# Sums moved from VectorE to GpSimd, the first product begun earlier, and the first pair of token blocks without sums

## The chip, the cores and the metric

The kernel runs on one core of one Trainium2 chip. The metric is the device time of one execution in microseconds (us). The kernel before took 384.91 us in the median of its first three runs (384.22, 384.91 and 767.23; the 767.23 was the first of them, and why it was slow is not known).

## The reference

Two stages follow each other. Attention with a sigmoid in place of the softmax, on 8 batches of 12 heads, 448 positions and 64 columns:

```python
scores = scale * np.matmul(q, k.transpose(0, 1, 3, 2)) - np.log(S)
attn = 1.0 / (1.0 + np.exp(-scores))
x = np.matmul(attn, v)          # then (B, H, S, D) -> (B*S, H*D) = (3584, 768)
```

and a two-layer block on its result:

```python
h = x @ w_in                    # 768 -> 2048, "product one"
g = h * np.cos(h)
out = g @ w_out                 # 2048 -> 768, "product two"
```

## The kernel before

TensorE does the scores, attention times v (AV) and both products. ScalarE does sigmoid and cosine. VectorE brings everything out of PSUM, multiplies h by its cosine, and makes copies of layouts. GpSimd only issues the loads, which cast float32 to float16 on the way.

Product two is done by a scheme with seven products for each pair of token blocks instead of eight. It needs four sums of quarters of w_out, once, and four sums of quarters of g for each of 14 pairs of blocks (a "quad" in the code). All of them are made on VectorE:

```python
def tt(out, in0, in1, op):
    nc.vector.tensor_tensor(out=out, in0=in0, in1=in1, op=op)

def dve_gsum(i, n):                        # 128x1024, fp16, four per quad
    a11, a12, a21, a22 = g_quarters(i)
    s1, s2, s4 = g_sum
    if n == 0:   tt(s1, a21, a22, ALU.add)
    elif n == 1: tt(s2, s1, a11, ALU.subtract)
    elif n == 2: tt(a21, a11, a21, ALU.subtract)
    else:        tt(s4, a12, s2, ALU.subtract)

def dve_wsum(n): ...                       # 128x3072, fp16, four in all
```

Other instructions of VectorE read SBUF:

```python
def dve_dup(s, y):                         # second half of x, 64x896 fp16, partitions swapped
    x = xts[s % N_X]
    nc.vector.tensor_copy(out=x[64 - 64 * y : 128 - 64 * y, 1], in_=x[64 * y : 64 * y + 64, 0])

def dve_il(s, i):                          # k and q with two heads interleaved, 128x896 fp16
    nc.vector.tensor_copy(out=ri.rearrange("p j y d -> p y j d"), in_=raw)

def dve_g(b, fp, part, hslot, cslot):      # g = h * cos(h): 128x768 and smaller pieces
    nc.vector.tensor_tensor(out=..., in0=hss[hslot]..., in1=css[cslot]..., op=ALU.mult)
```

The order of the instructions on each engine is not written by hand. The program contains a small model of the engines, with a duration for each kind of job; it plays the kernel through and puts the next job on whatever engine is free in the model. Constants at its top steer it. So a change of one duration, or of the engine of one sum, reorders what follows.

## Time and profile before

| kernel before | |
|---|---|
| time, median | 384.91 us |
| span of the profiled run | 382.6 us |
| TensorE, VectorE, ScalarE, GpSimd busy | 96, 76, 66, 17% |
| first product one, first product two | 26.85 us, 97.8 us |
| real work of TensorE, priced in the prediction | 347.1 us |

A multiplication of g takes 0.95 us (128x768; 55 of them, 52.4 us).

Throughout I speak of TensorE's *lost time*: the time passed less the real work done, priced with the unit costs of the prediction (0.0473 us for a 64x448 matmul, 0.1645 for a 128x384 one).

### The profile page before, as it was taken

What the parts mean: (1) busy time and instruction counts of PE and PEld (TensorE: products, weight loads), DVE (VectorE), ACT (ScalarE), POOL (GpSimd) and SP (SyncE); (2) the same over time, 40 slices, a digit from 0 to 9 for tenths busy, and PEclk for the clock granted to TensorE, in tenths of its full rate; (3) what the DMA queues carried; (4) which work ended last, traced back from release to release, by engine and by line L of the source; (5) the groups of instructions that cost most, each with busy time, mean ns of one, the idle gap of its engine ahead of it and who ended that gap; (6) DMA issues with size and microseconds to landing.
All of it is one profiled execution on the core that took longest, in us unless ns stands there. A gap on an engine that the chain in (4) does not pass through costs nothing. (4 is left out here: it accounts for less than half of the span.)

```text
span 382.6 us, 12691 instructions
## 1 busy us (share of the span) xinstructions
PE 368.7 (96%) x5577; PEld 233.8 (61%) x5577; DVE 289.2 (76%) x492; ACT 252.9 (66%) x260; POOL 66.9 (17%) x101
## 2 busy tenths in 40 slices
PE   8999997989999999999999999999999999999995
PEld 5556664666566565576665765565666555565553
DVE  2437588999877966967969788648789987779662
ACT  4997999798958688779488880389599660134000
POOL 8676331221022022030120202020000000000000
PEclk9999998999999999999999999999999999999999
DMA  8999999599869999598499956659510303210333
GB/s 165 197 197 199 215 204 201 85 153 97 126 105 169 114 121 136 116 163 115 79 177 165 133 75 120 144 67 130 109 27 2 68 18 75 53 43 2 84 82 82
DMA packets 69894, 44.14 MB, mean 115 GB/s; under 512 B 32464, under 2 KB 69840, under 8 KB 69840
## 3 DMA queue, kind: packets, MB, share of 16 engines
q0 software_dynamic: 29936, 22.48, 44.6%
q1 hardware_dynamic: 39824, 20.76, 29.3%
q8 instruction: 43, 0.70, 0.8%
q14 instruction: 11, 0.09, 0.1%
q10 hardware_dynamic: 80, 0.10, 0.1%
HBM read 45.61 MB, written 11.01 MB: 148 GB/s over the span
## 5 line engine op out<-in xcount | busy, mean ns | idle before, releaser
L253 ACT ACTIVATE sig<-pr,lgs_t 128x896 f16<-128x896 f32 x168 | 156.2, 1014 | 63.4 <-PE pr L244 60.7
L309 PEld LDWEIGHTS <-wi 64*64 64x64 f16 x3072 | 100.3, 107 | 48.5 <-issue 6.9
L309 PE MATMUL pr<-xt,wi 64*64 64x448 f16 x2048 | 117.3, 351 | 3.6 <-DVE xt L282 2.4
L326 ACT ACTIVATE cs<-hs,pih_t 128x896 f16<-128x896 f32 x63 | 61.7, 1033 | 32.3 <-DVE hs L323 30.9
L348 DVE TENSOR_TENSOR g_ring<-hs,cs 128x128 f16<-128x128 f32 (+1 forms) x134 | 74.4, 591 | 3.4 <-ACT cs L326 3.0
L412 PEld LDWEIGHTS <-g_ring 128*128 128x128 f16 x448 | 42.8, 98 | 34.1 <-issue 6.9
L244 PE MATMUL pr<-qT,kT 64*64 64x448 f16 x672 | 59.6, 356 | 2.7 <-DVE hs L323 1.5
L323 DVE COPY hs<-pr 128x896 f32<-128x896 f32 x42 | 45.7, 1088 | 21.8 <-PE pr L309 19.1
L412 PE MATMUL bk<-wo,g_ring 128*128 128x384 f16 x336 | 59.5, 327 | 1.0 <-DVE stage L358 0.9
L309 PE MATMUL bk<-xt,wi 64*64 64x448 f16 x1024 | 60.3, 349 | 0.0
L412 PEld LDWEIGHTS <-gs 128*128 128x128 f16 x336 | 32.8, 98 | 22.1 <-issue 0.4
L177 POOL DMA_DIRECT2D vt<-in_v_dram x21 | 14.9, 709 | 174.3 <-PE pr L270 157.1
L412 PE MATMUL bk<-ws,gs 128*128 128x384 f16 x224 | 41.0, 326 | 0.0
L244 PEld LDWEIGHTS <-kT 64*64 64x64 f16 x672 | 25.1, 106 | 18.2 <-issue 7.0
L323 DVE COPY hs<-bk 128x448 f32<-128x448 f32 x42 | 24.3, 616 | 11.4 <-PE bk L309 11.4
L280 DVE CAST xt<-pr 128x896 f16<-128x896 f32 x19 | 20.7, 1089 | 11.6 <-PE pr L270 11.4
L358 DVE TENSOR_TENSOR stage<-bk,p 128x384 f32<-128x384 f32 x42 | 23.3, 554 | 7.0 <-PE bk L412 6.8
L270 PE MATMUL pr<-sig,vt 64*64 64x448 f16 x476 | 26.0, 350 | 0.0
L270 PEld LDWEIGHTS <-vt 64*64 64x64 f16 x588 | 18.8, 107 | 8.9 <-issue 0.6
L412 PE MATMUL bk<-ws,g_ring 128*128 128x384 f16 x112 | 20.5, 326 | 0.1
L412 PE MATMUL bk<-wo,gs 128*128 128x384 f16 x112 | 20.5, 326 | 0.0
L358 DVE TENSOR_TENSOR stage<-bk,stage 128x384 f32<-128x384 f32 x28 | 15.5, 553 | 5.4 <-PE bk L412 5.3
(61 smaller groups left out, 248.9 us busy)
## 6 DMA issues: line engine op xcount, KB each, us to landing
out_dram<-stage SPq DMA_DIRECT2D x111, 96.0 KB, 2.2
vt<-in_v_dram POOLq DMA_DIRECT2D x21, 224.0 KB, 4.8
kraw<-in_k_dram POOLq DMA_DIRECT2D x19, 224.0 KB, 5.5
qraw<-in_q_dram POOLq DMA_DIRECT2D x19, 224.0 KB, 6.8
wo<-in_moe_w_out_dram POOLq DMA_DIRECT2D x4, 768.0 KB, 14.1
xt<-xt SPq DMA_DIRECT2D x20, 112.0 KB, 5.7
wi<-in_moe_w_in_dram POOLq DMA_DIRECT2D x16, 128.0 KB, 7.2
wi<-in_moe_w_in_dram POOLq DMA_DIRECT2D x4, 256.0 KB, 8.0
```

The source lines that it names most:

```text
L177: nc.gpsimd.dma_start(out=vt_of(s), in_=v[b, 4 * g : 4 * g + 4].rearrange("(y x) (p j) d -> (x p) y (j d)", y=2, j=NJ),)
L244: nc.tensor.matmul(out=pairs[wd][64 * x : 64 * x + 64, y, 0:S], lhsT=kT[64 * y : 64 * y + 64, x, PT * j : PT * j + PT], rhs=qT[64 * y : 64 ...
L253: nc.scalar.activation(out=sgs[slot], in_=pairs[wd][:, :, 0:S], func=AF.Sigmoid, bias=lgs_t, scale=0.125,)
L270: nc.tensor.matmul(out=two(wd)[x][64 * y : 64 * y + 64, 0:S], lhsT=vt[64 * x : 64 * x + 64, y, D * j : D * j + D], rhs=sgs[slot][64 * x : ...
L280: nc.vector.tensor_copy(out=out, in_=pairs[wd][r0:r1, :, 0:S])
L309: nc.tensor.matmul(out=two(wd)[r][64 * m : 64 * m + 64, 0:S], lhsT=w_in_sb[c][64 * r : 64 * r + 64, h, 128 * f + 64 * m : 128 * f + 64 * m ...
L323: nc.vector.tensor_copy(out=out, in_=src)
L326: nc.scalar.activation(out=css[cslot], in_=hss[hslot], func=AF.Sin, bias=pih_t, scale=1.0)
L348: nc.vector.tensor_tensor(out=out.rearrange("p n e t -> p e n t"), in0=hss[hslot][:, :, t : t + w].rearrange("p e (n t) -> p e n t", t=min ...
L358: nc.vector.tensor_tensor(out=out, in0=in0, in1=in1, op=op)
L412: nc.tensor.matmul(out=banks[bk][:, 0:HD], lhsT=lhs[:, kk, :], rhs=rhs[:, kk, :], start=first and kk == 0, stop=kk == HF - 1, skip_group_c ...
```

## The change

Its intent has three parts. Product one of batch 0 starts over the first four heads as soon as these are there (more half jobs, w_in's pieces loaded earlier, AV in smaller pieces). The first pair of token blocks is multiplied by eight plain products, so product two can begin before the sums of w_out exist. And the sums go to GpSimd, in pieces of 128x768 for w_out and 128x512 for g, to free VectorE. A list of hand-set picks (PE_PICK, DVE_PICK) goes with it. The core of the diff:

```diff
-    M2_AT = [13, 21, 26, 31, 35, 39, 37, 45, 55, 56, 56, 64, 64, 62]
+    M2_AT = [30, 8, 22, 58, 44, 53, 14, 44, 56, 62, 59, 46, 61, 57]
-    LOADS = 'q1 v0 q2 b0 v2 v1 y1 y0 q3 x0 b1 x1 ...'
+    LOADS = 'v0 q1 y2 x0 x1 q2 v1 v4 y1 q3 y0 x2 ...'
-    N_PLAIN = 0
+    N_PLAIN = 1
-    DUP_DVE = 3
+    DUP_DVE = 4
-    HALF1 = 4
-    HALF3 = 3
-    HALF_MAX = 3
+    HALF1 = 8
+    HALF3 = 8
+    HALF_MAX = 6
+    W_POOL = True
+    W_PIECES = 4
+    G_POOL = (1, 2, 3)
+    PE_PICK = {9: 's', 28: 'm', 69: 'm', ...}
+    DVE_PICK = {62: 1, 135: 1, 153: 0, 283: 1}
-    WARM_END = 40.0
+    WARM_END = 90.0
 ... (cut)
+    def gsum(eng, i, n, m, parts):
+        k = slice(HF * m // parts, HF * (m + 1) // parts)
 ...
+        eng.tensor_tensor(out=out, in0=in0, in1=in1, op=op)
 ...
+    def pool_wsum(n, m):
 ...
+        nc.gpsimd.tensor_tensor(out=out, in0=in0, in1=in1, op=ALU.subtract)
 ...
+            if n in G_POOL:
+                for m in range(2):
+                    pool_q.append((..., lambda i=i, n=n, m=m: gsum(nc.gpsimd, i, n, m, 2), fin if m else None))
+            else:
+                dve_q.append((0, 0.61, lambda i=i, n=n: gsum(nc.vector, i, n, 0, 1), fin))
 ... (rest of the generator cut)
```

## The prediction

> **What bounds the kernel now.** I read the totals per engine first, then the slices, then TensorE's instructions in order of time.
>
> ```profile
> PE 368.7 (96%) x5577; PEld 233.8 (61%) x5577; DVE 289.2 (76%) x492; ACT 252.9 (66%) x260; POOL 66.9 (17%) x101
> PE   8999997989999999999999999999999999999995
> ACT  4997999798958688779488880389599660134000
> POOL 8676331221022022030120202020000000000000
> PEclk9999998999999999999999999999999999999999
> PE 35%; DVE 1%; issue 0%
> ```
>
> TensorE is busy nearly throughout and the chain that ended last is almost all TensorE. But "busy" counts pipelined ends and filler multiplications on the identity, so I ask instead what TensorE's real work costs. The chain, listed in order of time, gives the step from one matmul to the next:
>
> ```profile
> 251.33 1.32 PE pr L270 x28
> 259.32 9.21 PE bk L412 x56
> 308.89 1.14 PE bk L309 x24
> ```
>
> So 0.0472 us for attention times v and for product one (L309), the same for the scores (0.19 us for 4), and 9.21/56 = 0.1645 us for product two. A transpose pair in the timeline takes 0.52 us for 14. Real work: 3072 x 0.0473 + 672 x 0.0473 (scores) + 672 x 0.0472 + 784 x 0.1645 + 252 x 0.037 = 145.3 + 31.8 + 31.7 + 129.0 + 9.3 = 347.1 us. The span is 382.6 us, so some 35.5 us of TensorE are lost. Laying these costs along the timeline, I find them (to about 1 us) at: 5.0 before 5 us; 10.8 from 5 to 30 us; 1.0 from 30 to 60; 8.1 from 60 to 95; 5.4 from 95 to 378 (265 us almost without a hole); 4.3 in the tail (last eviction and store). Only the second and the fourth are worth much.
>
> 5 to 30 us: ScalarE is the limit. It does one sigmoid per 0.93 us, and per sigmoid TensorE has only its scores (0.19), its AV piece (0.19) and a share of transposes (0.15) to do; product one first appears at 26.85 us. 60 to 95 us: one hole and its aftermath, then one wait:
>
> ```profile
> 62.52 1.12 PE L309 MATMUL pr<-xt,wi 64*64 64x448 f16 x8 [2.35 <-DVE xt L282]
> 63.57 0.96 PE L201 MATMUL bk<-ident,kraw 128*64 128x128 f16 x14
> ...
> 84.59 0.38 PE L244 MATMUL pr<-qT,kT 64*64 64x448 f16 x4 [1.47 <-DVE hs L323]
> ...
> 62.50:66.00 3.50, 3.43 (x48) 2.12 (x51) 3.44 (x8) 3.27 (x4) 1.12 (x2) 0.53 1.27 202
> ```
>
> The reader sees a cast of x that stood behind multiplications of g on VectorE, TensorE idle for 2.35 us, then 3.5 us at a granted clock of 0.53 in which 14 transposes take 0.96 instead of 0.58 us. VectorE is busy for 34.72 of these 35 us: it holds four sums of w_out (1.75 us each) and the first sums of g. The wait at 84.59 stands behind one of those 1.75 us sums (78.66 to 80.4 us) and what piled up after it.
>
> **What the Trainium skill says.** "TensorE: Matmul & The Clock Gate", Part 1: TensorE falls to half clock after an idle window of about 3.4 us and needs about as much busy time to come back. The lines above agree: 2.35 us idle after thin work, then 3.5 us at 0.53. "GPSIMD Engine Reference", section 3: a two-input elementwise add of 2048 columns takes 4497 ns on GpSimd, twice VectorE. The trace before has no such instruction, so it can't agree or disagree; scaled, I estimate 1.2 us for 512 columns and 1.8 us for 768. "SBUF — State Buffer", Who interferes with whom: a VectorE instruction with two SBUF inputs, or a copy in a two-port mode, and a GpSimd instruction that reads SBUF exclude each other for the whole instruction. No run shows this yet; it is the main danger here.
>
> **The change part by part**, with the instruction order of the changed kernel built but not run.
>
> 1. Earlier product one. w_in's first pieces are loaded before later k, q and v; AV is done in small pieces; 8 instead of 4 jobs of batch 0 may start on the first four heads. In issue order the first product one now follows the 11th score instead of the 22nd, that is near 17 us instead of 26.85. Counting real work issued before the same score (ScalarE sets the pace here, so the same score is about the same time), the new order is 2.3 us ahead at scores 19 to 29 and 3.0 us at score 31. I take 3 us (of the 5.3 us lost from 15 to 30 us). Price on VectorE: 16 more copies or adds of half results, 0.62 us each, 10 us, in 20 to 60 us, where VectorE is 72% busy.
>
> 2. Sums of w_out on GpSimd: 4 x 1.75 = 7.0 us off VectorE exactly in 70 to 82 us, where it is full. 16 pieces of estimated 1.8 us = 29 us on GpSimd, which is 17% busy. The 1.47 us wait should go.
>
> 3. First pair of blocks by eight plain products: 8 more matmuls, 8 x 0.1645 = +1.3 us of TensorE. In return product two can begin before the sums exist: in the issue order after the 55th score with 13 jobs of product one done, before it was after the 68th with 17. This gives TensorE 10.5 us of work without VectorE's h copies just where it starved. With fillers now allowed to 90 us the clock should not fall either. Of the 8.1 us lost from 60 to 95, I expect 5 back.
>
> 4. Three of four g sums on GpSimd: 13 x 3 x 0.685 = 26.7 us, plus 2.7 for the pair that needs none, off VectorE. 78 pieces of 1.2 us = 94 us on GpSimd. TensorE did not wait for these sums except 0.44 us between the last quads (the eviction stands behind sums). So in the middle there is nearly nothing to win, and a new cost: the g multiplications (about 80 us on VectorE), the remaining sum (9), and the re-layout copies of q and k (11.7) want the port that GpSimd's 94 + 29 us of adds hold. GpSimd holds it some 40% of 85 to 375 us; each of about 145 such VectorE instructions then waits 0.4 x 0.6 us = 0.25 us, together 36 us of VectorE, which eats the 36 us saved. VectorE's load stays near 76%, but its delays are lumpier: an eviction of PSUM can now stand behind a 0.95 us multiplication that stands behind an add. I charge 2 us of new TensorE waits to the middle. At the end, five quads follow closely; with s1 done 1.2 us after product 5 (fifth of seven), s2, a21 and s4 come 2.4 us apart, s2 about when product 6 of the next quad wants it. That costs 0 to 0.5 us a quad in place of the 0.44.
>
> 5. Table loads of ScalarE rise from 26 to 34 (8 x 1.28 = 10 us). Up to score 42 both orders have the same two bursts of four cosines, and later ScalarE has slack (66% busy). I charge nothing.
>
> Sum: -3 (early) -5 (60 to 95) +1.3 (plain) +2 (port) = -4.7 us sure-footed; the warm clock and lighter VectorE make other small waits in 95 to 378 us (5.4 us) shrink, for which, and because such a list of hand-set picks in the diff looks tuned to a result, I add -3.5. 384.9 - 8.2 = 376.7 us.
>
> **Rivals.** (a) The port lock bites: adds delay the g multiplications, h buffers come free late, and TensorE, whose order is fixed, waits 1 us and more in each of 14 quad periods. For: VectorE at 93% or so between quads (per job of product one 1.09 + 0.95 + 0.29 us against 2.3 us of TensorE). Against: hs has 5 buffers and quads give VectorE time to catch up. Time: 382 to 390. (b) The loads don't come in time: the first w_in pieces displace q and k (at 200 GB/s the queues are full until 60 us), scores starve, the early gain vanishes: 380 to 383. (c) Both early holes close wholly and VectorE's relief shows in the middle: 10.8 + 8.1 can't go to zero before 15 us, but 4.5 + 7 + 3 - 1.3 gives 371 to 372.
>
> **Range and chances.** The sum leans on two stretches whose gain I know to about 2 us each and on a port cost of 0 to 6 us. So 370.5 to 384. The 2% line is at 377.2, right by the centre; slower by 2% needs rival (a) at over 1 us a quad.
>
> **What would show it.** Early: first product one near 17 us; the first cosine burst, now at 44.3 us, one to three us sooner. 60 to 95: clock 1.00 in every window, no wait over 1 us, first product two near 75 us instead of 97.8. Sums: GpSimd's adds at 1.2 and 1.8 us; if they show 2 us or the 128x768 multiplication rises from 0.95 to over 1.3 us, the lock is real. Middle: TensorE's lost time from 95 to the end of its work at 5 to 8 us. The prediction is wrong if the first hole stays, if TensorE waits for GpSimd inside quads, or if the lock costs over 6 us.

## More of the kernel before

The loads stand in GpSimd's own queue, in front of or behind whatever else that engine has:

```python
def load_v(s):
    nc.gpsimd.dma_start(out=vt_of(s), in_=v[b, 4 * g : 4 * g + 4].rearrange(...))
```

Up to 60 us the kernel before has lost 16.8 us, up to 100 us 25.0, up to 140 us 26.4.

The prediction shows the totals, the slices and TensorE's waits. What it does not show is the groups of VectorE's instructions by form. The columns are line, engine, operation, output and inputs, their sizes, count, then busy time and mean ns of one, then idle time before them:

```profile
L348 DVE TENSOR_TENSOR g_ring<-hs,cs 128x768 f16<-128x768 f32 x55 | 52.4, 953 | 1.6 <-ACT cs L326 1.6
L289 DVE COPY xt<-xt 64x896 f16<-64x896 f16 x28 | 12.8, 456 | 0.6
```

## The result, and the profile after

The changed kernel is correct and takes 428.35 us in the median of four runs (427.57 to 429.07). The kernel before in the same rounds took 384.71 us (the median of four with the 767.23 among them; 384.51 without it). The ratio is 1.1139, with a 95% interval of 1.1108 to 1.1169. Ratios are computed from the mean time of one kernel's runs over the mean of the other's of the same rounds, so they are not quite the ratio of the medians quoted beside them. Executions over 1.5% slower than the fastest of the same kernel are left out of the means. The change made the kernel 43.6 us slower; the prediction was 376.7 us.

The page of the changed kernel, in the views that the prediction opened with (totals, slices, and the share of the chain that ended last):

```profile
PE 379.6 (89%) x5576; PEld 237.0 (56%) x5576; DVE 322.9 (76%) x469; ACT 265.2 (62%) x268; POOL 192.0 (45%) x199
PE   8999999919729988999879969899999798999996
POOL 8776410933590936092532530826003407054472
PEclk9999999959888999999989999999999899999999
PE 14%; DVE 2%; issue 1%; ACT 0%; DVEq 0%; ACTq 0%
```

A slice is 10.7 us. TensorE has one with a tenth of work in it (85 to 96 us) and another, with 2 tenths, at 117 to 128 us; its row before had no digit below 7 but the last. These stand at GpSimd's first long trains of sums. VectorE lost 23 of its 492 instructions and yet is busy 33.7 us longer. The chain that ended last covers 17% of the span, where it covered 36% before, and TensorE's part of it falls from 35 to 14%.

The chain in order of time shows that the unit costs of TensorE did not change (9.21/56 = 0.1645 us) and what stands between:

```profile
357.11 1.14 DVE xt L296
358.26 1.25 DVE xt L296
...
370.73 9.21 PE bk L426 x56
```

Two copies of x, which took 0.46 us on average before, take 1.14 and 1.25 us and release the next product.

VectorE's groups by form, to be read against the two lines of the kernel before:

```profile
L355 DVE TENSOR_TENSOR g_ring<-hs,cs 128x768 f16<-128x768 f32 x53 | 58.8, 1109 | 0.4 <-ACT cs L333 0.3
L296 DVE COPY xt<-xt 64x896 f16<-64x896 f16 x40 | 48.6, 1214 | 0.9
```

The copies went from 12.8 to 48.6 us, far more than the 12 added ones explain, and the multiplications went from 0.953 to 1.109 us each. A mean hides which copies these are. The instructions in order of time tell it; first TensorE's, then VectorE's, then GpSimd's, around the empty slice (the columns are start, length, engine, line, operation, count, and in brackets the idle time before it and its releaser):

```profile
79.63 5.38 PE L441 MATMUL bk<-wo,g_ring 128*128 128x384 f16 x32
94.03 6.18 PE L441 MATMUL bk<-wo,g_ring 128*128 128x384 f16 x26 [9.02 <-DVE stage L450]
```

```profile
76.55 1.16 DVE L330 COPY hs<-bk 128x448 f32<-128x448 f32 x2
77.73 11.90 DVE L296 COPY xt<-xt 64x896 f16<-64x896 f16 x2
89.67 0.39 DVE L236 COPY ri<-kraw 128x896 f16<-128x896 f16 x1
```

```profile
77.07 0.71 POOL L148 DMA_DIRECT2D qraw<-in_q_dram  x1
77.78 6.44 POOL L409 TENSOR_TENSOR ws<-wo,wo 128x768 f16<-128x768 f16 x4
84.18 4.81 POOL L409 TENSOR_TENSOR ws<-wo,ws 128x768 f16<-128x768 f16 x3
```

GpSimd issues the last of three loads and then makes seven sums of w_out without a gap, until 89.0 us. A pair of copies that VectorE begins at 77.73 us ends at 89.63. The next copy within SBUF, of 128x896 and with GpSimd idle, takes 0.39 us. Behind the pair, in VectorE's queue, stands the eviction (the copy of a finished product out of PSUM) that would free a PSUM bank, so TensorE does one burst of plain products at 79.63 us and then stands still for 9.02 us. The windows (length, busy time and count of TensorE, its weight loads, VectorE, ScalarE, GpSimd, then granted clock, share of the transfers and GB/s) show the aftermath:

```profile
80.00:90.00 10.00, 5.01 (x31) 2.91 (x30) 9.96 (x4) 4.03 (x5) 8.99 (x6) 0.87 0.16 23
90.00:100.00 10.00, 5.97 (x26) 3.09 (x26) 8.81 (x18) 4.23 (x4) 0.00 (x0) 0.61 0.49 85
```

The clock, which the change wanted to keep up in just this stretch, falls to 0.61. Two more holes of this kind follow: 2.69 us at 111.38 us, behind a pair of copies of 6.35 us, and 7.90 us at 128.02 us, behind a pair of 11.1 us, of which one copy takes 10.7. TensorE's lost time goes from 21.1 us (up to 80 us) to 46.9 us (up to 140 us), and from there it creeps to 73.8 us (up to 400 us), where the kernel before has 29.8 at 360 us. The creeping part looks different. Here is VectorE, and TensorE behind it, beside the sums of g of one quad (the middle pair of GpSimd's six sums takes 3.03 us there, against 2.27 us where VectorE leaves it alone):

```profile
213.00 3.06 DVE L355 TENSOR_TENSOR g_ring<-hs,cs 128x128 f16<-128x128 f32 x2
```

```profile
217.11 0.57 PE L251 MATMUL pr<-qT,kT 64*64 64x448 f16 x4 [2.70 <-DVE hs L330]
```

The group is a multiplication of 128x128 and one of 128x768, which take 1.24 and 1.90 us here; the means before are 0.29 and 0.95 us. Each is longer by 0.95 us, a little less than one sum (1.14 us where nothing disturbs it). TensorE waits 2.70 us for the h copy behind them.

### The profile page after: what moved, and what is told of

Read it like the earlier page. It is cut to its first block, busy times and chain, and to the rows that moved or that the text cites. A ratio compares the mean times of both kernels' runs of the same rounds, so it can differ in the third digit from the quotient of the medians.

```text
span 427.0 us, 12797 instructions
## 1 busy us (share of the span) xinstructions
PE 379.6 (89%) x5576; PEld 237.0 (56%) x5576; DVE 322.9 (76%) x469; ACT 265.2 (62%) x268; POOL 192.0 (45%) x199
## 5 line engine op out<-in xcount | busy, mean ns | idle before, releaser
L260 ACT ACTIVATE sig<-pr,lgs_t 128x896 f16<-128x896 f32 x154 | 145.3, 1010 | 62.5 <-PE pr L251 62.3
L316 PE MATMUL pr<-xt,wi 64*64 64x448 f16 x1856 | 106.7, 353 | 2.3 <-DVE xt L296 1.4
L355 DVE TENSOR_TENSOR g_ring<-hs,cs 128x128 f16<-128x128 f32 (+2 forms) x130 | 90.5, 728 | 1.4 <-ACT cs L333 1.2
L390 POOL TENSOR_TENSOR gs<-gs,g_ring 128x512 f16<-128x512 f16 x26 | 33.1, 1288 | 121.2 <-DVE gs L390 81.3
L316 PE MATMUL bk<-xt,wi 64*64 64x448 f16 x1216 | 73.9, 356 | 10.3 <-DVE xt L296 7.9
L251 PE MATMUL pr<-qT,kT 64*64 64x448 f16 x672 | 63.7, 360 | 13.6 <-DVE hs L330 11.1
L330 DVE COPY hs<-pr 128x896 f32<-128x896 f32 x37 | 40.2, 1087 | 19.8 <-PE pr L316 19.4
L296 DVE COPY xt<-xt 64x896 f16<-64x896 f16 x40 | 48.6, 1214 | 0.9
L330 DVE COPY hs<-bk 128x448 f32<-128x448 f32 x48 | 27.6, 617 | 12.5 <-PE bk L316 12.5
L390 POOL TENSOR_TENSOR g_ring<-g_ring 128x512 f16<-128x512 f16 x26 | 32.2, 1256 | 0.0
L390 POOL TENSOR_TENSOR gs<-g_ring,gs 128x512 f16<-128x512 f16 x26 | 32.1, 1252 | 0.0
L277 PE MATMUL pr<-sig,vt 64*64 64x448 f16 x476 | 30.3, 360 | 0.0
L365 DVE TENSOR_TENSOR stage<-bk,p 128x384 f32<-128x384 f32 x39 | 21.6, 553 | 9.2 <-PE bk L426 8.6
```

What stands on the lines that cost most here:

```text
L251: nc.tensor.matmul(out=pairs[wd][64 * x : 64 * x + 64, y, 0:S], lhsT=kT[64 * y : 64 * y + 64, x, PT * j : PT * j + PT], rhs=qT[64 * y : 64 ...
L260: nc.scalar.activation(out=sgs[slot], in_=pairs[wd][:, :, 0:S], func=AF.Sigmoid, bias=lgs_t, scale=0.125,)
L277: nc.tensor.matmul(out=two(wd)[x][64 * y : 64 * y + 64, 0:S], lhsT=vt[64 * x : 64 * x + 64, y, D * j : D * j + D], rhs=sgs[slot][64 * x : ...
L316: nc.tensor.matmul(out=two(wd)[r][64 * m : 64 * m + 64, 0:S], lhsT=w_in_sb[c][64 * r : 64 * r + 64, h, 128 * f + 64 * m : 128 * f + 64 * m ...
L330: nc.vector.tensor_copy(out=out, in_=src)
L355: nc.vector.tensor_tensor(out=out.rearrange("p n e t -> p e n t"), in0=hss[hslot][:, :, t : t + w].rearrange("p e (n t) -> p e n t", t=min ...
```

## The experiments

The question is where 43.6 us come from. Theory "port": VectorE and GpSimd keep each other from SBUF, so VectorE's copies and multiplications wait for sums. Rival "order": the new order of instructions is bad in itself. Rival "late sums": sums of GpSimd take twice as long, and product two waits for them. Three words recur. A *train* is a row of sums on GpSimd without a pause. An instruction *asks* at its recorded start; if it must wait after that, the wait is a part of its recorded duration. It is *held* if it waits for more than the sum that is running. All runs in the following table are correct.

| run | what it is | us | ratio to before, 95% interval |
|---|---|---|---|
| same_order | order of after, all sums on VectorE | 386.74 | 1.0044, 1.0011 to 1.0077 |
| same_w | order of after, only w_out sums on GpSimd | 408.89 | 1.0643, 1.0626 to 1.066 |
| same_g | order of after, only g sums on GpSimd | 403.81 | 1.054, 1.0495 to 1.0586 |
| same_w_small | same_w, a small add behind loads | 405.55 | 1.0559, 1.0537 to 1.0582 |
| same_w_wait | same_w, a real wait behind loads | 397.32 | 1.0326, 1.0308 to 1.0343 |
| small_add | after, a small add behind loads | 425.84 | 1.1073, 1.1037 to 1.111 |
| psum_dup | order of after, second half of x from PSUM | 457.10 | 1.1856, 1.1793 to 1.1919 |
| w_on_dve | generated again, w_out sums on VectorE | 421.42 | 1.0938, 1.09 to 1.0976 |
| g_on_dve | generated again, g sums on VectorE | 420.27 | 1.0896, 1.0847 to 1.0945 |
| no_pool | generated again, all sums on VectorE | 397.69 | 1.0337, 1.0294 to 1.038 |
| early_only | only the early start | 393.58 | 1.0219, 1.0186 to 1.0251 |
| before_plain | before, first pair by plain products | 396.57 | 1.0308, 1.0254 to 1.0362 |
| before_pool | before, all but s1 on GpSimd | 431.72 | 1.1209, 1.1167 to 1.1252 |
| before_wpool | before, only w_out sums on GpSimd | 412.31 | 1.0717, 1.063 to 1.0804 |
| before_gpool | before, only g sums on GpSimd | 439.69 | 1.1419, 1.1338 to 1.1501 |

### same_order: is it the order or the engine?

Every instruction stays where the changed kernel has it; the 94 pieces are only issued on the other engine.

```diff
-        nc.gpsimd.tensor_tensor(out=out, in0=in0, in1=in1, op=ALU.subtract)
+        nc.vector.tensor_tensor(out=out, in0=in0, in1=in1, op=ALU.subtract)
-  ... gsum(nc.gpsimd, i, n, m, 2) ...
+  ... gsum(nc.vector, i, n, m, 2) ...
```

> The changed kernel with every instruction in its place, but the 94 sums of w_out and g that went to GpSimd are issued on VectorE. Theory (port): the changed kernel loses its time because VectorE's copies and multiplications stand behind whole trains of GpSimd adds; then the long copies of x (6 to 12 us in the trace) and TensorE's holes of 9.0, 7.9 and 2.7 to 3.5 us go, against some 35 us of sums added to VectorE: 378 to 392 us. Rival (order): the new order of loads and products is itself bad; then at least half of the 43 us stays: over 405 us.

It took 386.74 us, 0.4% over before. The rival "order" falls: 41.6 of the 43.6 us come with the engine of the sums. The run also shows what the other two parts of the change are worth. TensorE is as busy as before:

```profile
PE 371.3 (96%) x5576; PEld 232.7 (60%) x5576; DVE 304.0 (79%) x563; ACT 264.7 (69%) x268; POOL 69.2 (18%) x105
```

Its lost time is 20.1 us up to 60 us (before 16.8), 21.3 up to 100 us (25.0), and 24.9 up to 140 us (26.4). So the hole of 60 to 95 us is gone, as meant, and 3.2 us more are lost before it. There VectorE is busy 27.2 of the 30 us from 30 to 60 us, where it was busy 21.6 before: the extra half results of product one fill it.

### w_on_dve and g_on_dve: one kind of sums at a time, generated again

```diff
 w_on_dve:
-    W_POOL = True
+    W_POOL = False
 g_on_dve:
-    G_POOL = (1, 2, 3)
+    G_POOL = ()
```

> Changed kernel, sums of w_out back on VectorE (scheduled anew), g sums still on GpSimd. Port: the three trains of 128x768 adds go, and with them the holes from 80 to 130 us, about 23 us; the holes of 2 to 3.5 us behind g sums stay: 398 to 410. Order: over 418.

> Changed kernel, g sums back on VectorE (scheduled anew), w_out sums still on GpSimd. Port: the holes after 140 us go (about 15 to 20 us), those from 80 to 130 us stay: 402 to 418. Order: over 418.

They took 421.42 and 420.27 us, both above what I expected for the port, and both in the range that I had set for the rival "order" (over 418). So by their times alone they would speak for the rival; same_order, where the order is held fixed, is the run that decides. The costs do not add up to 41.6 us (36.5 and 35.4 us over before), but the order of the two differs from that of the changed kernel, so this says little about the sum. What they do show is the long copies, each with only one kind of sum there. In g_on_dve the same three pairs of copies take 11.9, 6.35 and 11.1 us, with the same holes of 9.01, 2.69 and 7.90 us. In w_on_dve a copy of 6.03 us stands behind six sums of g of 128x512, so the width of 768 is not needed.

### before_pool: the sums alone, on the kernel before

The generator of the changed kernel gets back every constant of the kernel before, except these two:

```diff
+    W_POOL = True
+    G_POOL = (1, 2, 3)
```

> The kernel before with only the engine of the sums changed (w_out's four and three of g's four on GpSimd), nothing else of the change. Port: slower than before though its order of loads and products is the old one: 400 to 430. Order: within 2% of before (378 to 392).

It took 431.72 us, 47 us over before and just over the range of the port theory. The other parts of the change are not needed for the loss. Its longest copy, 9.53 us at 83.54 us, is an interleaving copy of k, not a copy of x, and a multiplication of 128x128 takes 7.29 us at 126.33 us. One caution that the expectations of this run and of two later ones lack: the two engines' durations in the model differ, so from about a quarter of the program on TensorE's order is not that of the kernel before.

### port_probe: what a sum does to one instruction of VectorE

A kernel (its output is zeros) with scenes in which ScalarE releases both engines at once: GpSimd starts seven sums of 128x512, VectorE a few instructions of one kind.

```diff
+    for m in range(train):
+        nc.gpsimd.tensor_tensor(out=po_all[:, m], in0=pa, in1=pb, op=ALU.add)
+    for m in range(ops):
+        nc.vector.tensor_copy(out=x[64:128, 1], in_=x[0:64, 0])
```

> Wrong result on purpose (writes zeros). Scenes: VectorE does 64x896 fp16 SBUF copies, 128x768 fp32 x fp16 multiplications of two SBUF inputs, PSUM copies, or PSUM+SBUF adds, alone and against a train of seven GpSimd adds of 128x512; in other scenes each GpSimd add waits for its forerunner's semaphore, or for a ScalarE copy in between. Port, train form: the copy takes the whole rest of the train, 6 to 8 us instead of 0.45; the multiplication too or at least one add longer; PSUM copies and PSUM+SBUF adds stay as they are alone (within 10%). Port, one-add form (what the prediction assumed): no VectorE instruction is longer than its own time plus one add, 1.3 us. Rival, no port at all: nothing changes. With waits between the adds: if the lock is held by back-to-back adds only, the copy ends after one add, below 2 us.

A copy alone takes 0.39 us. Two against a train take 0.83 and 1.22 us, so each gets in after one sum. Eight multiplications of 128x768 take 13.42 us, where alone two took 1.94, and the seven sums beside them 12.09 instead of 7.81 us: they alternate, each waiting for one instruction of the other. Eight PSUM copies (5.23 us) and eight adds of PSUM and SBUF (5.77 us) are not touched. In the scenes with all sums on one tile, or with a wait for ScalarE after each sum, VectorE waits for one sum as well (1.22 us at most for a copy, 1.79 for a multiplication). So the exclusion is shown for itself, but not a wait for a whole train. The kernel had something that the probe lacked.

### no_pool, early_only and before_plain: the parts without GpSimd

```diff
 no_pool (from after):         early_only (from after):       before_plain (from before):
-    W_POOL = True             as no_pool, and                -    N_PLAIN = 0
-    G_POOL = (1, 2, 3)        -    N_PLAIN = 1               +    N_PLAIN = 1
+    W_POOL = False            +    N_PLAIN = 0
+    G_POOL = ()               PE_PICK, DVE_PICK = {}, {}
```

> Changed kernel with all sums on VectorE, scheduled anew: early start, plain products and picks alone. By the prediction's own sum for these parts (3 + 5 less 1.3 us) it is faster than before by 7 us, 378. If VectorE, full from 30 to 60 us in the changed kernel, eats the early gain: 382 to 388.

> Changed kernel with all sums on VectorE, no plain products, no hand-set picks: the early start of product one and its loads alone. Prediction's step 1: 3 us faster, 382. If the 16 extra half results on VectorE eat it: 384 to 390.

> Kernel before with the first pair of blocks by eight plain products and nothing else. Costs 1.3 us of TensorE; if beginning product two sooner fills the holes of 60 to 95 us: 380 to 383; if the holes stay: 385 to 387.

All three miss: 397.69, 393.58 and 396.57 us, while the order of the changed kernel with the same sums on VectorE takes 386.74. My reading, which no run tests, is that the picks and thresholds fit one order of jobs and are here applied to another. Against the best order at hand (same_order, or the kernel before) 7 to 12 us are lost (early_only loses 6.4 us between 40 and 60 us, before_plain 9.2 us between 100 and 120 us). No part alone is faster than before. And differences of 10 us between programs that were generated anew are not a measure of one edit, so I went back to fixed orders.

### before_wpool and before_gpool: where each kind loses its time

```diff
 before_wpool, against before_pool:    -    G_POOL = (1, 2, 3)   +    G_POOL = ()
 before_gpool, against before_pool:    -    W_POOL = True        +    W_POOL = False
```

> The kernel before, with only the four sums of w_out issued on GpSimd (16 pieces of 128x768). Before with all sums on GpSimd took 431.7 us, 46.7 over before, and had holes of 8.71, 2.38 and 6.54 us on TensorE behind VectorE copies that waited for trains of these pieces. Port theory: those holes come with the w_out sums alone: 398 to 412 us, a copy of over 6 us in the trace, granted clock back at 1.0 after 160 us. Rival, late sums: what costs is that product two waits for sums that GpSimd gives later; then the waits of TensorE name GpSimd and no VectorE instruction is long: 388 to 395 us. If it is under 388, the w_out sums on GpSimd cost nothing by themselves and the two kinds only hurt together.

> The kernel before, with only three of four sums of g of each pair of blocks issued on GpSimd (128x512 pieces). Port theory: 24 to 30 us over before by about one add of waiting for each product of g that stands beside a train, so 405 to 420 us, with the 128x768 multiplication 1.1 us or more in the mean and no single copy over 3 us in the first 120 us, because the trains of w_out pieces are absent. Rival, late sums: VectorE's durations stay as before (0.95 us for the multiplication), TensorE's waits name GpSimd: 390 to 400 us. The costs of the two kinds should add up to about the 46.7 us of both; if both together are clearly more or less than that, each makes room for the other or takes it.

before_wpool took 412.31 us, at the top of its range. TensorE loses 40.3 us between 60 and 140 us and under 0.8 us in each later 20 us. Its largest holes:

```profile
104.20 0.59 PE L251 MATMUL pr<-qT,kT 64*64 64x448 f16 x4 [9.18 <-DVE hs L330]
...
126.14 0.96 PE L316 MATMUL bk<-xt,wi 64*64 64x448 f16 x8 [6.55 <-DVE xt L296]
```

Both stand behind copies of x (10.39 us for a pair, 6.92 us for one) that waited for a train of six and one of four sums. A third hole, of 5.89 us at 73.81 us, stands behind a multiplication of 128x768 that took 6.41 us beside a train of three.

before_gpool took 439.69 us, far over both theories, and more than both kinds together. The mean of the 128x768 multiplication is 0.967 us, only 0.014 over before. What is new is that TensorE waits for GpSimd itself, five times over 1 us (1.77 to 4.00, together 14.8 us):

```profile
312.17 2.74 PE L426 MATMUL bk<-ws,gs 128*128 128x384 f16 x8 [4.00 <-POOL gs L390]
```

So in this order the "late sums" rival is right for 14.8 of the 55.0 us; where the rest goes was not followed up. In the order of the changed kernel, in its own trace and in that of same_g, no wait of TensorE of over 0.1 us names GpSimd, so there the rival falls. The costs of the two kinds (27.6 and 55.0 us) do not add up to the 46.8 us of both; these three programs differ in their order, so nothing follows from it.

### psum_dup: take the reason for waiting away from the longest copies

The probe showed PSUM copies untouched. So the second half of x is written from PSUM as well, right after the first. TensorE's, ScalarE's and GpSimd's order stays that of the changed kernel.

```diff
     def dve_AV(s, wd, part):
         copy_two(xts[s % N_X][:, 0], wd, part, 0, 128)
+        if by_dve[s]:
+            for y in range(2):
+                copy_two(xts[s % N_X][64 - 64 * y : 128 - 64 * y, 1], wd, part, 64 * y, 64 * y + 64)
     def dve_dup(s, y):
-        nc.vector.tensor_copy(out=x[64 - 64 * y : 128 - 64 * y, 1], in_=x[64 * y : 64 * y + 64, 0])
+        pass
```

> The changed kernel in its own order on TensorE, ScalarE and GpSimd, with one edit: the second half of x is no longer copied within SBUF (64x896, two per unit) but written from the same PSUM banks as the first half, by two more PSUM copies of 64x896 or 64x448 right after it. The probe showed PSUM copies untouched by a train of GpSimd adds. Port theory: the copies of 11.9, 6.35 and 11.1 us and TensorE's holes of 9.02, 7.90 and 2.69 us behind them are gone; VectorE pays about 20 pairs x (2 x 1.0 - 0.8) = 24 us more of busy time, a part of which is on the path in the full stretch of 30 to 60 us. Multiplications and the interleaving copies of k and q still wait. So 402 to 420 us instead of 428, and the holes of over 6 us only if an interleaving copy meets a train. Rival: the copies are long because VectorE waits for something else than the port (its own operands, a semaphore), then the PSUM copies in their place are long too and the time is 425 to 440 us.

It took 457.10 us, far from the 402 to 420 that I expected, and above the rival's 425 to 440. The new PSUM copies themselves are not held (1.09 us for 64x896, as for 128x896), so the rival's reason falls too. But the wait has only moved to the next instruction that reads SBUF, an interleaving copy of k:

```profile
127.02 8.58 DVE L236 COPY ri<-kraw 128x896 f16<-128x896 f16 x1
```

There are two such copies (the other takes 9.36 us at 92.14 us), with TensorE holes of 7.28 and 4.35 us. And the PSUM copies hold their banks longer: TensorE waits 1.2 to 2.4 us for the first half of x more than ten times. My estimate of their price was low as well: 48 copies of 1.09 or 0.62 us take 44.8 us of VectorE, where the 40 copies within SBUF would take 15.6 at 0.39 us each without waits. An instruction that is exempt does not help while the one after it in the queue is not.

### port_probe2: a train behind loads

In the kernel each long copy stood beside a train that follows a load in GpSimd's queue. The second probe adds that, in scenes with four copies each:

```diff
+    for g in range(gens):
+        nc.gpsimd.dma_start(out=ld[:, g], in_=src.rearrange(...))      # casting load, as in the kernel
     for m in range(train):
         nc.gpsimd.tensor_tensor(...)                                  # 128x768 or 128x512
```

> Wrong on purpose (the output is zeros): isolated scenes, as in the first probe, with what it had left out. Wide adds of 128x768, a chain of adds on one tile, three casting loads issued by GpSimd ahead of seven adds with VectorE's four copies of 64x896 beginning 2, 3 or 4 PSUM copies (0.58 us each) later, the same with 128x512 adds, and the 128x896 copy that interleaves k and q. Theory A, the load issues decide: a copy that asks while GpSimd makes the descriptors of a load, with adds queued right behind, gets the port only after the whole train, so the scenes with loads show a copy of 8 to 12 us and those without show 0.8 to 1.7 us (one add of 768 columns is 1.6 us). Theory B, the width decides: the scenes with 768 columns show the long copies, with or without loads, and those with 512 columns do not. Theory C, neither: all scenes show one add per copy, and the long waits of the kernel need something that the probe lacks (traffic of other engines on SBUF).

The view of one source line lists the copies of each scene, with shortest, median and longest in ns ("gtrain" is three scenes):

```profile
L64 DVE COPY x_gtrain<-x_gtrain x12: 387/390/14045, 44.5 to 98.1; 64x896 f16<-64x896 f16 x12
...
L64 DVE COPY x_wide<-x_wide x4: 1430/1708/1729, 5.8 to 10.7; 64x896 f16<-64x896 f16 x4
```

Without loads ("wide") no copy takes more than 1.73 us, one sum of 768 columns. With loads ahead of the same train the first copy takes 14.0, 13.4 and 12.7 us in the three scenes, that is until the seven sums (11.2 us) and a memset of 2.0 us behind them are over, and the others 0.39 us. It does not matter whether the copy asks during the load issue or in the first sum. Sums on one and the same tile ("chain", 1.73 us at most) change nothing, and the interleaving copy behaves alike (12.7 us with loads, 1.7 without). The scenes with 512 columns agree only in part: the copy that asked in the first sum waited 8.13 us, the one that asked during the load issue took 0.89 us. So a train behind loads holds a copy in five scenes of six, and B and C fall. The condition that theory A named, asking during the load issue, is not what decides: three of the five asked in the first sum, and the one that was not held asked during the issue.

### port_probe3: what ends the hold

> Wrong on purpose (zeros). Scenes as in the second probe, three casting loads issued ahead of seven adds of 128x768 unless said otherwise, and VectorE's first operation asking in the first or second add. (one) a single load ahead of the train: if any load issue starts the hold, the first copy takes over 9 us. (wait) a small add that waits for ScalarE stands between loads and train: if an idle GpSimd gives the port back, copies alternate again, 1.6 to 1.7 us each; if not, one of over 9 us. (small) the same small add without a wait: the hold stays, over 9 us. (gap) every add is followed by one that waits for ScalarE: copies at most 3 us. (behind) five adds first and the loads behind them: copies at 1.7 us until the loads. (mult) multiplications with two SBUF inputs instead of copies: the first waits for the train like the copy, over 9 us; the rival is that they only alternate (1.7 us), as in the changed kernel, where no multiplication took over 1.9 us. (psum) PSUM copies: 0.62 us each, untouched. (again, third) the 128x512 scene that alternated in the second probe, asked for 2 and 3 PSUM copies after the release: if the asking time within the load issue decides, one of them alternates and the other holds.

```diff
     loads(gens)
+    if between == "wait":   # ScalarE works for some time; GpSimd's small add waits for it
+        nc.gpsimd.tensor_tensor(out=po[:, 0, 0:8], in0=w[:, 0:8], in1=go, op=ALU.add)
+    elif between == "small":
+        nc.gpsimd.tensor_tensor(out=po[:, 0, 0:8], in0=go, in1=go, op=ALU.add)
     for m in range(train): ...
```

```profile
L77 DVE COPY x_one<-x_one x4: 387/388/12074, 9.2 to 22.1; 64x896 f16<-64x896 f16 x4
L77 DVE COPY x_wait<-x_wait x4: 799/1708/1728, 29.3 to 33.6; 64x896 f16<-64x896 f16 x4
L77 DVE COPY x_small<-x_small x4: 401/1708/1731, 45.5 to 49.4; 64x896 f16<-64x896 f16 x4
...
L79 DVE TENSOR_TENSOR x_mult<-h,c x4: 957/959/11995, 97.5 to 111.5; 128x768 f16<-128x768 f32 x4
```

A single load is enough ("one", 12.1 us). A GpSimd that has waited for ScalarE gives way after each sum ("wait"), and so does one with a small add in between ("small"), where I had expected a hold. Multiplications are held as well (12.0 us, against 1.79 at most beside the train of the first probe); this one did not wait for the memset behind the train, as the copies did. PSUM copies are not (eight in 5.23 us), and a train ahead of its loads alternates (1.73 us at most). Where each sum is followed by a wait for ScalarE ("gap") no copy takes over 1.86 us. One more hold stands at the end of the scene with PSUM copies: a copy of 128x8 that asked in the fifth sum waited 6.43 us, for the rest of the train and the memset, where the same copy in the scenes "wait" and "small" took 1.60 us. So to ask late does not help. Both 512-column scenes, which asked during the load issue, alternate, as one did in the second probe. I expected one of the two to hold.

### same_w and same_g: the two kinds in the fixed order

same_w takes only the second edit of same_order, same_g only the first.

> The changed kernel's order, w_out sums on GpSimd, g sums issued on VectorE. All sums on VectorE in this order took 386.7 us, all on GpSimd 428.4. Theory hold: three holes of some 20 us together and a few us of low clock behind them: 406 to 414 us, all of the loss between 60 and 140 us. Rival: the w_out sums cost little without the g sums: under 400 us.

> The changed kernel's order, g sums on GpSimd, w_out sums issued on VectorE. If the costs add up, what same_w leaves of the 41.6 us: 400 to 410 us, with TensorE's lost time spread over 140 to 340 us in pieces of 1 to 4 us, multiplications of 128x768 at 1.1 us, and one long copy where a g train stands behind loads. If it is under 395, most of the loss of the g sums came from the shifts that the w_out holds made.

They took 408.89 and 403.81 us, both in the range. Over same_order that is 22.2 us for the sums of w_out and 17.1 us for those of g, and both together 41.6: in one order the costs nearly add up (39.2). The runs were spread over several chips; by the ratios to the kernel before of the same rounds they add up fully (6.0 and 5.0% against 10.95%). In same_w TensorE has the three holes of the changed kernel (9.02, 2.69 and 7.90 us), and loses 25.7 us between 80 and 140 us, where same_order loses 3.4. In same_g no train of w_out sums exists, the loss is spread in holes of 0.8 to 3.5 us from 115 us on, none of them named after GpSimd, one copy of x is held for 4.18 us by a train of g sums behind loads, and VectorE's durations show where it comes from:

```profile
L355 DVE TENSOR_TENSOR g_ring<-hs,cs 128x768 f16<-128x768 f32 x53 | 58.7, 1107 | 0.4 <-ACT cs L333 0.3
```

In same_order the mean is 949 ns. The excess is 53 x 0.158 = 8.4 us, for the 61 small multiplications 61 x 0.144 = 8.8, for 40 copies of x 4.6 and for 30 interleaving copies 5.2 us, together 27 us. The sums that went away had durations of 32 us, but neighbours overlap by some 0.08 us each: VectorE is busy 304.0 us in same_order and 304.9 us here, so the waits ate all that was saved.

### small_add and same_w_small: a small add behind the loads

```diff
+    def small_add():
+        if loaded[0]:
+            nc.gpsimd.tensor_tensor(out=tiny[:, 0], in0=tiny[:, 1], in1=tiny[:, 1], op=ALU.add)
+        loaded[0] = False
```

It is called before each sum on GpSimd; every load sets loaded. All other instructions stay in order.

> The changed kernel with one edit: between a load issue and the next sum on GpSimd stands an add of 128x8 on a tile of its own (0.2 us, no wait). In the probe that made one copy of 12.7 us into copies of 1.4 us. Theory hold: the copies of 11.9, 6.35 and 11.1 us and the TensorE holes of 9.02, 2.69 and 7.90 us behind them are gone (none over 3 us in 60 to 140 us), and the time falls from 428 to 403 to 413 us. Rival, coincidence of the probe (the asking time): holes stay, 423 to 430 us.

> As same_w, with the small add behind load issues. Theory hold: the loss of same_w mostly goes: 388 to 396 us, copies at most 3.3 us (two adds). Rival (holes have another cause): as same_w within 3 us.

They took 425.84 and 405.55 us: 2.5 and 3.3 us gained, not the 13 to 25 that I expected. Two of the three long copies remain, and this line of small_add shows why the probe misled me:

```profile
78.55 12.06 DVE L310 COPY xt<-xt 64x896 f16<-64x896 f16 x2
```

The third load is issued from 77.88 to 78.59 us, the small add from 78.59 on. The copy asked at 78.55, during the load issue; in the probe it had asked during the small add itself. So a small add that follows without a pause is no remedy. What the scene "small" showed was its asking time.

### same_w_wait: GpSimd made to wait behind the loads

```diff
             nc.gpsimd.tensor_tensor(out=tiny[:, 0], in0=tiny[:, 1], in1=tiny[:, 1], op=ALU.add)
+            nc.scalar.copy(out=tiny[:, 2], in_=tiny[:, 0])
+            nc.gpsimd.tensor_tensor(out=tiny[:, 3], in0=tiny[:, 2], in1=tiny[:, 2], op=ALU.add)
```

> As same_w (408.9 us; 386.7 with these sums on VectorE), with a handshake between load issues and the next w_out sum: a small add on GpSimd, a copy of its result by ScalarE, and a second small add that waits for the copy, so GpSimd stands idle for some 0.5 to 2 us before each of the three trains. Theory hold: no copy over 3.5 us, no TensorE hole over 3 us between 60 and 140 us, 389 to 398 us. Rival (the hold does not depend on what stands between loads and train; or the long copies have another cause): a copy of over 6 us stays, 402 to 411 us.

It took 397.32 us, 11.6 us less than same_w, in the range of the theory, with one hole a little over the 3 us that I had set. GpSimd, then VectorE at the place of the first long pair:

```profile
76.75 0.39 POOL L151 TENSOR_TENSOR tiny<-tiny 128x8 f16<-128x8 f16 x1
80.38 0.22 POOL L153 TENSOR_TENSOR tiny<-tiny 128x8 f16<-128x8 f16 x1 [3.23 <-ACT tiny L152]
80.56 8.05 POOL L428 TENSOR_TENSOR ws<-wo,wo 128x768 f16<-128x768 f16 x4
```

```profile
76.70 0.79 DVE L312 COPY xt<-xt 64x896 f16<-64x896 f16 x2
```

The pair takes 0.79 us instead of 11.9 and asks, as before, in the last load. No copy within SBUF takes over 1.4 us beside a train, and the sums now show that VectorE gets in between them (8.05 us for four instead of 6.44). The holes are 3.4 us at most. The handshake does two things at once, though: it lets GpSimd stand idle, and by that (1.9 to 3.2 us each time) it moves each train later, past the copy that would have waited. The traces can tell the two apart. Inside its two longer trains eleven VectorE instructions that read SBUF asked, six and five, and none waited for more than one sum (2.39 us at most); in same_w each of the three trains held the copy that asked until the train was over.

The same count over all traces of whole kernels that have sums on GpSimd (trains of three sums or more, beside which VectorE wanted SBUF) tells the same without a probe:

| what stands right ahead of the train | trains | trains that held a VectorE instruction for two sums or more | longest such instruction |
|---|---|---|---|
| a load issue, no pause | 26 | 24 | 11.5 us |
| a load issue and a small add, no pause | 5 | 4 | 11.65 us |
| a pause or a wait of GpSimd (over 0.2 us) | 43 | 0 (of 152 instructions) | 2.59 us |

Programs of one order repeat the same trains, so these are not 26 cases independent of each other. The two exceptions in the first row and the one in the second are trains of 128x512. But 512 columns do not protect: in w_on_dve a copy that asked during the load issue at 271.38 us took 4.26 us, the whole train of three. The remaining 10.6 us over same_order go with one-sum waits: holes of 1.9, 2.9 and 3.4 us in 85 to 120 us behind evictions and h copies, and a granted clock of 0.71 from 118 to 128 us.

No version that I tried beats the kernel before. The nearest is same_order, 0.4% slower.

## Why the prediction was wrong

The step that failed is step 4, and with it the list of what step 2 costs. In the prediction's words, "GpSimd holds it some 40% of 85 to 375 us; each of about 145 such VectorE instructions then waits 0.4 x 0.6 us = 0.25 us" and "I charge 2 us of new TensorE waits to the middle". Two things were wrong in it.

**The longest wait.** It was taken as half a sum. Behind a load issue a copy waited for what was left of the train of sums, up to 11.7 us in the kernels (a pair of 12.06 less 0.39 for the one that is not held), and everything behind it in VectorE's queue waited too. Step 2 moved the sums of w_out to GpSimd "which is 17% busy" and charged no waits at all. And the list of VectorE instructions that want the port (multiplications of g, the remaining sum, the copies of q and k) left out the copies of x, in which all three long waits of the changed kernel lie. Measured in one order, moving the sums of w_out costs 22.2 us. Making GpSimd wait behind its loads brought 11.6 of them back. Why GpSimd gives way after each sum in one case and not in the other is not settled. What the probes show: of ten scenes with sums directly behind a load issue and VectorE reading SBUF, seven held (six with 768 columns, one with 512 that asked in the first sum), and three did not (512 columns, asking during the load issue). Where a wait stood between, or no load ahead of the train, GpSimd gave way after each sum. In the kernels all VectorE instructions of over 6 us, copies and two multiplications, stand at a train with a load issue right ahead (in small_add and same_w_small with the small add in between).

**From VectorE's time to TensorE's.** The prediction set 36 us of waits against 36 us saved on VectorE. That was right: same_g shows 27 us of waits, and VectorE's busy time hardly moves (304.0 to 304.9 us). What was wrong was to conclude that TensorE then loses 2 us; it loses 17.1. The sums that were removed had stood where TensorE did not wait for them, as step 4 had read itself, and the waits that replaced them stand in front of h copies and evictions, for which TensorE waits. A total of an engine that does not change can still cost time on the path.

The other steps:

- Step 1 predicted the first product one near 17 us; it came at 18.45 us. It charged nothing for the 10 us of half results on VectorE, which it named. In same_order the 3 us gained do not appear; 3.2 us more are lost by 60 us instead (20.1 against 16.8). That the half results are the reason fits VectorE's 27.2 of 30 us, but no run takes them away alone. The first cosine, which should have come sooner, came at 47.92 us against 45.64 before.
- Steps 2 and 3 predicted 5 us back between 60 and 95 us, at 1.3 us for the plain products. In same_order the stretch from 60 to 100 us loses 1.2 us instead of 8.2, with the clock at 1.00: right, and a little better. But same_order has all sums on VectorE, so this gain came without step 2: the 7.0 us that step 2 took off VectorE were not needed for it. The first product two came at 79.63 us, not near 75. In the changed kernel the hold of GpSimd fell into the very same stretch.
- The 3.5 us added because the list of picks "looks tuned to a result" had no mechanism behind it and came to nothing: the order with all sums on VectorE is 1.8 us slower than before, where steps 1 to 3 and this guess added up to -10.2 us.
- Step 5, table loads at no charge: not tested by itself. same_order has them too and costs 1.8 us in all.

The sum by measured terms, in the order of the changed kernel: order +1.8, sums of w_out +22.2, sums of g +17.1, both together a further +2.4: with rounding 43.4 of the 43.6 us, in place of -8.2. The +2.4 is what is left over between medians of different rounds; by the ratios it is nothing. Rival (a) named the port but at "1 us and more in each of 14 quad periods" and 382 to 390 us. Its two signs were set for the average case: the sums took 1.25 to 1.29 and 1.63 to 1.65 us, and the multiplication 1.11 us (under the 1.3 us at which I would have believed the lock), and the loss was in three copies that neither sign looks at. "The prediction is wrong if ... the lock costs over 6 us" is what happened. Two smaller readings are loose. By the durations beside it, rival (a)'s "VectorE at 93% or so" is 2.33 against 2.3 us, which is full; 93% holds only if the overlap of neighbours is taken off. And the lines that are said to agree with a half clock after some 3.4 us of idling show 2.35 us idle, then 3.5 us at 0.53: the clock agrees, the idle time is shorter.

The Trainium skill, "SBUF — State Buffer", section Who interferes with whom, had it right that the loser blocks fully, and that "Issue order, not op shape, decides who blocks." The runs agree for single instructions (0.39 against 0.83 to 1.22 us). I used it as an average over instructions that start at random.

## What to carry to other kernels

Before moving elementwise work to GpSimd, list which VectorE instructions read SBUF (here copies within SBUF and instructions with two SBUF inputs were held, copies out of PSUM and adds of PSUM and SBUF were not) and what stands behind them in VectorE's queue; a wait there is paid by everything behind. Do not let a train of GpSimd arithmetic follow its own load issues without a pause: here one copy then waited 12 us instead of 1.7. And when a generated order is tuned, test a change of engine with the order held fixed, since programs generated anew were slower by 7 to 12 us without any sum on GpSimd.

## What the Trainium skill lacked or had wrong

- "SBUF — State Buffer", Who interferes with whom, says that the pair is held for the whole instruction. It lacks that a train of GpSimd sums directly behind a load issue can hold it for the whole train: one copy of 64x896 took 12.1 to 14.0 us there (a memset of 2.0 us behind the train included) and 1.7 us at most without the load issue, and a multiplication of two SBUF inputs 12.0 us against 0.96 us alone. In the kernels 24 of 26 such trains held, and none of 43 that began after a pause.
- The same section warns of VectorE keeping GpSimd from writing descriptors. The other direction, a load issue that keeps VectorE waiting, is spelled out on no page that I read: a copy that asked during the second of three load issues, with no sum behind them, took 3.50 us instead of 0.39. It waited for the rest of the issues (1.2 us) and for a memset of 2.0 us right behind them; two copies that asked during the first issue took 0.39 and 0.42 us.
